# Chunked attention and mixture of experts on one core: one 512 KB load for q and k, earlier stores, routing steps moved behind the maximum

## The chip, the cores and the metric

The kernel runs on one core of a Trainium2 chip. A time is the device time of one execution in microseconds (us). The kernel before was timed three times: 364.58, 366.62 and 370.21 us, a median of 366.62 us.

## The reference

Attention works inside chunks of 64 tokens, for 8 batches, 8 heads, 576 tokens and a head width of 64. Its output, as 4608 rows of 512, goes through a mixture of experts in which every row picks one expert and may skip it:

```python
scores = scale * np.matmul(q_c, k_c.transpose(0, 1, 2, 4, 3))      # 64 x 64 in each chunk
scores = scores - np.max(scores, axis=-1, keepdims=True)
attn = np.exp(scores)
attn = attn / (np.sum(attn, axis=-1, keepdims=True) + 1e-09)
out = np.matmul(attn, v_c)
x = out.transpose(0, 2, 1, 3).reshape(B * S, H * D)                # 4608 x 512

do_compute = x @ w_skip > 0
xc = x[do_compute]
logits = xc @ w_gate                                               # 8 experts
e_idx = np.argmax(logits, axis=1)
gate_w = softmax(logits)[np.arange(len(xc)), e_idx]
for e in range(8):
    mask = e_idx == e
    h = np.maximum(xc[mask] @ w1[e], 0.0)                          # 512 -> 1024
    y[mask] = gate_w[mask, None] * (h @ w2[e])                     # 1024 -> 512
out = x.copy(); out[do_compute] = xc + y
```

## The kernel before, in words

**Attention** works on 36 tiles of 128 rows. The loop over `i` (line 611) is a software pipeline written out by hand: one turn issues a stage of several tiles. TensorE's order in a turn is: transpose of x of tile i-3 (`pe_xtrans`, L282), transpose of the probabilities of tile i-1 (`pe_ptrans`, L244), subtraction of the row maximum for tile i (`pe_sub`, L232, two matmuls that read `mx`), logits of tile i-4 (`pe_logits`, L310 and L311, which read `xh`), matmuls of the routing, scores of tile i+1 (`pe_scores`, L220, 32 matmuls), and probabilities times v of tile i-1 (`pe_pv`, L259, 32 matmuls into `pv`). The PSUM tile `pv` has a single buffer, and so has the bank `xt`.

VectorE normalizes tile i-2 (`ve_norm`: L266, L268, L270, which writes x and thereby frees `pv`), sums the logits (`ve_logits`, L320), does routing steps, and takes the maximum over the scores of tile i+1 (`ve_max`, L226). ScalarE copies the transposed x to `xs` (L294), and GpSimd splits `xs` into the two float16 halves `xh` (a cast, L296, and a subtraction, L297). An engine executes its instructions in the order in which they are written; a wait holds up everything behind it on the same engine.

**Transfers** go through SyncE's one queue, in the order written: q and k of tile i+4 (`load_q`, `load_k`, 256 KB each, into the two halves of one tile `qk`), v (`load_v`, 260 KB), the store of a finished tile of x (`store`, L276), and 16 halves of the first expert's weights (`load_half`, L461) at the turns in `W_TILES`. A load is held back until TensorE has reached a given stage (`paced`), so that transfers keep step with the tiles. The list `others` holds the weight half and the stores of a turn; its length limit (L614) says how many stores a turn may issue.

**Routing** runs on groups of 14, 9 and 13 tiles (`GS`). `route` is a generator whose steps wear a letter and an estimated length: "d" steps are VectorE's, "p" TensorE's, "r" VectorE's reading of a TensorE result. `run_route("d", budget)` issues "d" steps until the budget is spent. The steps make one-hot rows (`oh`, L401, three tiles at a time, beside them `rv` on GpSimd) and in the end, in `finish_records`, the row numbers `reci` (L439).

**Early gathers.** When the first two groups (tiles 0 to 22) are routed and stored, `early_fetch` lets GpSimd gather the first three blocks of rows of the first expert from the output in HBM (`gather`, L475, an indirect DMA each). The gathers wait for `reci` and for the landing of the stores of tiles 0 to 22; the store of tile 22 is the last of them.

**The experts** follow: the first expert's layer 1 is spread over the end of attention (L496 with `pd`), then for each expert layer 1 (L496), layer 2 (L525), the scatter of the results, and the conversion of the next experts' weights to two float16 halves by ScalarE and VectorE (L742, L743).

Of the kernel before, what the change touches and what calls it, by code (L numbers as in the profile page):

```python
# [9 lines left out]
F32 = mybir.dt.float32  # L10
# [8 lines left out]
P = 128  # L19
B, H, S, D = 8, 8, 576, 64  # L20
CH = 64
NTOK = B * S
NT = NTOK // P
DM = H * D
# [13 lines left out]
GS = (14, 9, 13)  # L38
NG = len(GS)
GT = [(g, i, n) for g, n in enumerate(GS) for i in range(n)]  # L40
EARLY_G, EARLY_B = 2, 3
# [6 lines left out]
LOOK = 4  # L48
# [8 lines left out]
EARLY_I = NT - 2  # L57
# [37 lines left out]


@with_exitstack
def moe_attention_kernel(ctx: ExitStack, tc: tile.TileContext, q: bass.AP, k: bass.AP, v: bass.AP, cst: bass.AP, wall: bass.AP, out: bass.AP):
    nc = tc.nc
    halves = (slice(0, CH), slice(CH, P))  # L100

# [5 lines left out]
    ap = apool.__enter__()  # L107
# [8 lines left out]
    T = [dict() for _ in range(NT)]  # L116
# [4 lines left out]
    def paced(ins, at):  # L121
        if at in stage:
            dep = mybir.DependencyInfo(mybir.DependencyClass.Sync, mybir.DependencyReason.DATA)
            tc.add_manual_dep(getattr(ins, "ins", ins), stage[at].name, dep, reason="pace of the transfers")

    def reached(at, ins):
        stage[at] = getattr(ins, "ins", ins)

    def load_q(t, at=None):
        if t < NT:  # L130
            T[t]["qk"] = ap.tile([P, 2, DM], F32, name="qk", bufs=LOOK + 1)
            paced(nc.sync.dma_start(T[t]["qk"][:, 0], q[t]), at)

    def load_k(t, at=None, eng=None):
        if t < NT:
            paced((eng or nc.sync).dma_start(T[t]["qk"][:, 1], k[t]), at)

    def load_v(t, at=None):
        if t < NT:
            T[t]["v"] = ap.tile([P, 2 * KC * VW], F32, name="v", bufs=LOOK + 2)  # L140
            paced(nc.sync.dma_start(T[t]["v"], v[t]), at)

    csb = cpool.tile([P, CCOLS], F32, name="csb")
    load_q(0)
    load_k(0, eng=nc.scalar)
    load_q(1)
    load_k(1)
    load_v(0)
    nc.sync.dma_start(csb, cst)
    load_v(1)  # L150
    load_q(2)
    load_k(2)
    load_v(2)
    load_q(3)
    load_k(3)
    load_v(3)

    ones = cpool.tile([P, P], F16, name="ones")
# [36 lines left out]
    def more_constants():  # L195
        nc.vector.tensor_copy(upper, C("upper"))
        nc.vector.tensor_copy(iota, C("iota"))
        nc.vector.tensor_scalar(wgs[:, :, 0], wg, SR, None, op0=ALU.mult)
        nc.vector.scalar_tensor_tensor(wgs[:, :, 1], wg, SR, wgs[:, :, 0], op0=ALU.mult, op1=ALU.subtract)
        nc.gpsimd.tensor_copy(vals[:, :, 0], C("tok"))  # L200
        nc.gpsimd.tensor_copy(vals[:, :, 2], C("part").to_broadcast([P, NT]))
        nc.gpsimd.memset(ecum[:, 0, :], 0.0)
        nc.gpsimd.memset(rec, 0.0)
# [6 lines left out]


    def pe_scores(t):
        qk = T[t].pop("qk")
        sp = ps_s.tile([P, 2, DM], F32, name="sp")
        for j in range(KC):
            for c in range(2):
                for a in range(2):
                    h = (j % 2) * 4 + (j // 2) * 2 + a
                    w = slice(h * CH, (h + 1) * CH)
                    ins = nc.tensor.matmul(sp[halves[a], c, j * CH:(j + 1) * CH], qk[halves[c], 0, w], qk[halves[c], 1, w], start=(j == 0), stop=False, skip_group_check=True)  # L220
        T[t]["sp"] = sp
        reached("scores", ins)

# [49 lines left out]
    held = []  # L273
# [172 lines left out]
    def run_route(kinds, budget):  # L446
        while routes and routes[0][0][0] in kinds and budget > 0:
            budget -= routes[0][0][1]
            routes[0][0] = next(routes[0][1], None)
            if routes[0][0] is None:  # L450
                routes.pop(0)
# [87 lines left out]
    def on(f, t, *a):  # L539
        if 0 <= t < NT:  # L540
            f(t, *a)
# [26 lines left out]
    def early_xt(m, alloc):  # L568
        blk_xt(xt0[:, :, :, m * P:(m + 1) * P], xgs[m], P, alloc)
# [41 lines left out]
    for i in range(-1, NT):  # L611
        host.clear()
        others = [(load_half, m) for m, t in enumerate(W_TILES) if t == i]
        while held and len(others) < (1 if i < EARLY_I - 5 else 2 if i < NT - LOOK else 4):  # L614
            others.append((store, held.pop(0)))
        run_route("w", 1)
        on(pe_xtrans, i - 3)
        on(ve_norm, i - 2)
        on(ac_xs, i - 3)
        if 0 <= i - 2 < NT:  # L620
            held.append(i - 2)
        if i >= 0:
            on(load_q, i + LOOK, "x")
        on(pe_ptrans, i - 1)
        on(ac_pt, i - 1)
        on(pe_sub, i)
        on(ac_exp, i)
        if i >= 0:
            on(load_k, i + LOOK, "sub")
        on(pe_logits, i - 4)  # L630
        run_route("p", 1)
        on(ve_logits, i - 4)
        run_route("r", 1)
        run_route("d", 750 if i < sum(GS[:EARLY_G]) + 3 else 1000)
        if i in EARLY_AT:
            early_xt(EARLY_AT[i], xt_bank)
        on(pe_scores, i + 1)
        on(ve_max, i + 1)
        for n, (f, t) in enumerate(others):
            f(t, ("scores", None)[n > 0])  # L640
        on(pe_pv, i - 1)
        if i >= 0:
            on(load_v, i + LOOK, "pv")
        if i == 1:
            more_constants()
        if w_pend and (i > W_TILES[FC] or i < W_TILES[FC] and (len(w_pend) > 1 or i > W_TILES[FC - 1])):
            conv_half()
        while i == EARLY_I - 2 and len(ready) == 1:
            host.clear()
            run_route("w", 1)  # L650
            run_route("p", 1)
            run_route("rd", 1 << 30)
        if held and held[0] >= sum(GS[:EARLY_G]):
            early_fetch()
# [170 lines left out]
    for u, (p, bs, offs, n) in enumerate(units):  # L825
# [7 lines left out]
        w, hc = wsets[p], ht  # L833
# [8 lines left out]
        at = 0  # L842
# [57 lines left out]
def lay_out(q, k, v, moe_w_skip, moe_w_gate, moe_w1, moe_w2):  # L900
    nch = S // CH

    def cols(a):
        return np.ascontiguousarray(a.reshape(B, H, nch, CH, D).transpose(0, 2, 4, 1, 3)).reshape(NT, P, DM)


    vv = v.reshape(B, 2, KC, nch, CH, D).transpose(0, 3, 1, 4, 2, 5).reshape(NT, 2, P, KC, D).transpose(0, 2, 1, 3, 4)
    vv = np.concatenate([vv, np.ones((NT, P, 2, KC, 1), np.float32)], axis=4).reshape(NT, P, 2 * KC * VW)
    cst = constants()
    wsg = np.concatenate([moe_w_skip[:, None], moe_w_gate], axis=1)  # L910
    lo, hi = _C["wsg"]
    cst[:, lo:hi] = wsg.reshape(KC, P, NX).transpose(1, 0, 2).reshape(P, -1)
    w1 = moe_w1.reshape(NE, KC, P, FC, P).transpose(0, 3, 2, 1, 4).reshape(NE, FC, P, KC * P)
    w2 = moe_w2.reshape(NE, FC, P, DM)
    wall = np.ascontiguousarray(np.concatenate([w1, w2], axis=3))
    return {"in_q": cols(q), "in_k": cols(k), "in_v": np.ascontiguousarray(vv), "in_cst": cst, "in_wall": wall}


# [12 lines left out]
```

## Time and profile before

| | |
|---|---|
| median of three runs | 366.62 us (364.58 to 370.21) |
| the profiled execution | 364.89 us, its span 363.1 us |
| TensorE busy (PE) | 316.4 us, 87% of the span |
| VectorE (DVE) | 237.5 us, 65% |
| ScalarE (ACT) | 164.7 us, 45% |
| GpSimd (POOL) | 152.4 us, 42% |
| data moved | 81.82 MB, mean 225 GB/s |

All rows of this document come from one profiled execution. PE is TensorE, PEld its weight loads, DVE VectorE, ACT ScalarE, POOL GpSimd, SPq SyncE's queue. "L220" is a line of the kernel. In `[6.18 <-DMA out<-x]` the first number is the idle time of the engine just before the instruction, and behind the arrow stands what ended it; "issue" means that the profile shows nothing that was waited for. [...] Attention ends near 144 us of the span; the rest is the experts.

### The profile page before, as it was taken

To read this page: it belongs to the slowest core of one execution; us is meant where nothing else is said; L and a number is where in the kernel's file an instruction comes from. 1 tells how busy PE (TensorE), PEld (TensorE's weight loads), DVE (VectorE), ACT (ScalarE), POOL (GpSimd) and SP (SyncE) were. 2 spreads that over 40 slices of the span, in tenths; PEclk is the share of its full clock that TensorE was granted. 3 is DMA by queue.
4 is the path that set the end of the run, shared out by engine and by line. 5 is a ranking of instruction groups with operands and counts; after the bars stand their busy time and mean duration, and the time that the engine had idled before them with its cause. 6 is when DMAs were issued, how large, how long until landed. Compare 5 with 4: busy or idle time off the path is not lost.

```text
span 363.1 us, 11291 instructions
## 1 busy us (share of the span) xinstructions
PE 316.4 (87%) x4543; PEld 223.8 (62%) x4543; DVE 237.5 (65%) x526; ACT 164.7 (45%) x335; POOL 152.4 (42%) x179
## 2 busy tenths in 40 slices
PE   7698787788977559989999998999999999999991
PEld 3577676677866547654555543764755857668580
DVE  2455454689697426695556999786777867868320
ACT  2454355444554416424345744463654655456120
POOL 5145576769878287586120026134025023111111
PEclk9999899999999969999999999999999999999996
DMA  8999798989999857816751588767667668663000
GB/s 266 390 277 362 249 327 268 314 258 311 314 301 311 297 167 235 315 43 194 238 170 59 180 265 253 256 199 217 226 204 238 211 209 279 190 217 120 29 25 27
DMA packets 42471, 81.82 MB, mean 225 GB/s; under 512 B 5150, under 2 KB 5150, under 8 KB 42416
## 3 DMA queue, kind: packets, MB, share of 16 engines
q1 hardware_dynamic: 39168, 71.47, 59.9%
q0 software_dynamic: 3104, 9.33, 8.2%
q8 instruction: 37, 0.61, 0.7%
q10 hardware_dynamic: 144, 0.26, 0.2%
q14 instruction: 18, 0.15, 0.1%
HBM read 67.01 MB, written 14.17 MB: 224 GB/s over the span
## 4 chain that ended last, share of the span: by engine, by line
PE 69%; DVE 8%; POOL 6%; issue 5%; DMA 5%; ACT 4%; POOLq 0%; ACTq 0%
PE y L525 26%; PE hp L496 20%; PE sp L220 4%; PE xt L282 4%; PE pv L259 4%; ACT xs L294 3%; PE pd L496 3%; DMA qk<-in_k 3%; PE xq L488 2%; POOL xh L297 2%; PE xt L310 2%; DMA out<-x 2%; PE pt L244 1%; POOL rv L400 1%; DMA xg<-out,reci 1%
## 5 line engine op out<-in xcount | busy, mean ns | idle before, releaser
L525 PE MATMUL y<-wset,ht 128*128 128x512 f16 (+7 forms) x552 | 101.9, 379 | 0.0
L496 PEld LDWEIGHTS <-wset 128*128 128x128 f16 x864 | 73.5, 98 | 24.4 <-issue 3.8
L475 POOL DMA_INDIRECT out<-yo,reci x22 | 24.5, 1115 | 144.2 <-DVE yo L535 123.1
L496 PE MATMUL hp<-xt,wset 128*128 128x288 f16 (+6 forms) x768 | 81.1, 267 | 1.7 <-DVE ht L501 1.1
L525 PEld LDWEIGHTS <-ht 128*128 128x128 f16 (+7 forms) x552 | 45.6, 101 | 46.5 <-issue 2.0
L743 DVE SCALAR_TENSOR_TENSOR wset<-wst,wset 128x512 f16<-128x512 f32 x112 | 71.5, 683 | 1.4 <-ACT wset L742 0.5
L742 ACT ACTIVATE wset<-wst 128x512 f16<-128x512 f32 x112 | 62.9, 620 | 2.2 <-DMA wst<-in_wall 2.2
L500 ACT ACTIVATE ht<-hp 128x288 f16<-128x288 f32 (+6 forms) x64 | 23.5, 371 | 49.9 <-PE hp L496 49.4
L294 ACT ACTIVATE xs<-xt 128x512 f32<-128x512 f32 x33 | 19.7, 596 | 55.9 <-PE xt L282 55.9
L226 DVE TENSOR_REDUCE mx<-sp 128x8 bf16<-128x512 f32 x36 | 24.8, 688 | 25.7 <-PE sp L220 25.7
L501 DVE SCALAR_TENSOR_TENSOR ht<-hp,ht 128x288 f16<-128x288 f32 (+6 forms) x64 | 25.3, 405 | 23.1 <-ACT ht L500 22.0
L297 POOL TENSOR_TENSOR xh<-xs,xh 128x512 f16<-128x512 f32 x33 | 38.5, 1166 | 2.6
L296 POOL CAST xh<-xs 128x512 f16<-128x512 f32 x33 | 20.7, 626 | 32.2 <-ACT xs L294 32.2
L220 PE MATMUL sp<-qk 64*64 64x64 f32 x1152 | 26.7, 230 | 6.8 <-issue 5.8
L475 POOL DMA_INDIRECT xg<-out,reci x22 | 24.5, 1114 | 12.5 <-DMA out<-x 6.2
L259 PE MATMUL pv<-v,pts 64*64 64x65 f32 x1152 | 25.9, 222 | 4.4 <-issue 3.8
L489 ACT ACTIVATE xt<-xq 128x512 f16<-128x512 f32 (+7 forms) x19 | 9.6, 509 | 42.0 <-PE xq L488 42.0
L220 PEld LDWEIGHTS sp<-qk 64*64 64x64 f32 x1152 | 21.4, 139 | 9.9 <-issue 7.3
L270 DVE TENSOR_TENSOR x<-pv,rr 128x512 f32<-128x512 f32 x36 | 24.9, 691 | 1.4 <-DVE rr L268 0.2
L237 ACT ACTIVATE px<-sp 128x512 f32<-128x512 f32 x36 | 21.6, 600 | 8.9 <-PE sp L232 8.9
L259 PEld LDWEIGHTS pv<-v,pts 64*64 64x64 f32 x1152 | 21.9, 137 | 5.7 <-issue 4.6
L535 DVE SCALAR_TENSOR_TENSOR yo<-y,recg,xg 128x512 f32<-128x512 f32 (+7 forms) x23 | 17.1, 742 | 12.2 <-PE y L525 10.9
(122 smaller groups left out, 374.2 us busy)
## 6 DMA issues: line engine op xcount, KB each, us to landing
wst<-in_wall SPq DMA_DIRECT2D x128, 256.0 KB
v<-in_v SPq DMA_DIRECT2D x36, 260.0 KB
qk<-in_q SPq DMA_DIRECT2D x36, 256.0 KB
out<-x SPq DMA_DIRECT2D x36, 256.0 KB
qk<-in_k SPq DMA_DIRECT2D x35, 256.0 KB
xg<-out,reci POOLq DMA_INDIRECT x22, 4.1
out<-yo,reci POOLq DMA_INDIRECT x22, 3.4
qk<-in_k ACTq DMA_DIRECT2D x1, 256.0 KB
```

The costliest lines, as they stand in the source:

```text
L220: ins = nc.tensor.matmul(sp[halves[a], c, j * CH:(j + 1) * CH], qk[halves[c], 0, w], qk[halves[c], 1, w], start=(j == 0), stop=False, skip ...
L226: nc.vector.tensor_reduce(mx, T[t]["sp"][:, :, :KC * CH].rearrange("p c (j s) -> p c j s", s=CH), axis=AX.X, op=ALU.max, negate=True)
L259: ins = nc.tensor.matmul(pv[halves[c], jj, m * VW:(m + 1) * VW], pt[halves[jj], c * 2 + jp, halves[a]], vv[halves[jj], c * KC + m, :], sta ...
L270: nc.vector.tensor_tensor(x.rearrange("p (g m d) -> p g m d", g=2, m=KC), pv[:, :, :, :D], rr.unsqueeze(3).to_broadcast([P, 2, KC, D]), op ...
L294: nc.scalar.activation(xs, T[t].pop("xt"), AF.Copy, scale=SX)
L297: nc.gpsimd.tensor_tensor(xh[:, 1], xs, xh[:, 0], op=ALU.subtract)
L475: ins = nc.gpsimd.indirect_dma_start(**kw)
L496: nc.tensor.matmul(hp, w[:, a, fc, j * P:(j + 1) * P], xt[:, b, j, :n], start=(m == 0), stop=(m == 11))
L501: nc.vector.scalar_tensor_tensor(ht[:, 1, fc, :n], hp, 0.0, ht[:, 0, fc, :n], op0=ALU.max, op1=ALU.subtract)
L525: nc.tensor.matmul(y[c * P // cg:c * P // cg + n], ht[:, a, fc, o:o + n], w[:, b, fc, P * KC:], start=(f == 0 and m == 0), stop=(f == fw - ...
L742: nc.scalar.activation(w[:, 0, fc, r], st[part], AF.Copy, scale=SW)
L743: nc.vector.scalar_tensor_tensor(w[:, 1, fc, r], st[part], SW, w[:, 0, fc, r], op0=ALU.mult, op1=ALU.subtract)
```

## The change

Three edits. First, q and k lie in one input `in_qk` with q and k of a row side by side (4096 bytes), and `load_qk` loads both in one transfer of 512 KB, held back to the stage "sub", as k was; q was held back to the stage "x", somewhat earlier in the turn. Tile 0 is still loaded in two halves on two queues. Second, the limit of one item a turn in `others` ends at turn 26 instead of 29 (`EARLY_I - 8` for `EARLY_I - 5`, `EARLY_I` is 34). Third, `run_route("d", ...)` is called behind `ve_max` instead of ahead of `early_xt`, `pe_scores` and `ve_max`.

```diff
-    def load_q(t, at=None):
+    def load_qk(t, at=None):
         if t < NT:
             T[t]["qk"] = ap.tile([P, 2, DM], F32, name="qk", bufs=LOOK + 1)
-            paced(nc.sync.dma_start(T[t]["qk"][:, 0], q[t]), at)
-
-    def load_k(t, at=None, eng=None):
-        if t < NT:
-            paced((eng or nc.sync).dma_start(T[t]["qk"][:, 1], k[t]), at)
+            paced(nc.sync.dma_start(T[t]["qk"], qk[t]), at)
...
-    load_q(0)
-    load_k(0, eng=nc.scalar)
-    load_q(1)
-    load_k(1)
+    T[0]["qk"] = ap.tile([P, 2, DM], F32, name="qk", bufs=LOOK + 1)
+    nc.sync.dma_start(T[0]["qk"][:, 0], qk[0][:, 0])
+    nc.scalar.dma_start(T[0]["qk"][:, 1], qk[0][:, 1])
+    load_qk(1)
...
-        while held and len(others) < (1 if i < EARLY_I - 5 else 2 if i < NT - LOOK else 4):
+        while held and len(others) < (1 if i < EARLY_I - 8 else 2 if i < NT - LOOK else 4):
             others.append((store, held.pop(0)))
...
-        if i >= 0:
-            on(load_q, i + LOOK, "x")
         on(pe_ptrans, i - 1)
...
         if i >= 0:
-            on(load_k, i + LOOK, "sub")
+            on(load_qk, i + LOOK, "sub")
...
         run_route("r", 1)
-        run_route("d", 750 if i < sum(GS[:EARLY_G]) + 3 else 1000)
         if i in EARLY_AT:
             early_xt(EARLY_AT[i], xt_bank)
         on(pe_scores, i + 1)
         on(ve_max, i + 1)
+        run_route("d", 750 if i < sum(GS[:EARLY_G]) + 3 else 1000)
...
-    return {"in_q": cols(q), "in_k": cols(k), "in_v": ...
+    return {"in_qk": np.ascontiguousarray(np.stack([cols(q), cols(k)], axis=2)), "in_v": ...
```

**SyncE's queue, turns 28 to 31, before.** The numbers in the names tell buffers apart; `x_2062` is x of tile 22, `out_0` the output.

```order
L276 DMA out_0<-x_1615 128x512
L141 DMA v_2518<-in_v 128x520
L132 DMA qk_2539<-in_q 128x512
L136 DMA qk_2539<-in_k 128x512
L276 DMA out_0<-x_1718 128x512
L276 DMA out_0<-x_1809 128x512
L141 DMA v_2603<-in_v 128x520
L132 DMA qk_2621<-in_q 128x512
L136 DMA qk_2621<-in_k 128x512
L276 DMA out_0<-x_1896 128x512
L276 DMA out_0<-x_1979 128x512
L141 DMA v_2700<-in_v 128x520
```

The store of `x_2062` is still four rows further on, behind the loads of `qk_2718`. The same queue in the changed kernel, from turn 27 on, where x of tile 22 is `x_2035`:

```order
L455 DMA wst_2379<-in_wall 128x512
L270 DMA out_0<-x_1695 128x512
L137 DMA v_2399<-in_v 128x520
L132 DMA qk_2431<-in_qk 128x1024
L270 DMA out_0<-x_1785 128x512
L270 DMA out_0<-x_1871 128x512
L137 DMA v_2489<-in_v 128x520
L132 DMA qk_2521<-in_qk 128x1024
L270 DMA out_0<-x_1953 128x512
L270 DMA out_0<-x_2035 128x512
L137 DMA v_2573<-in_v 128x520
L132 DMA qk_2602<-in_qk 128x1024
```

The store of tile 22 is issued in turn 29 instead of turn 31, and a tile has one load for q and k.

**GpSimd, turns 30 to 33, before** (`xh_2715` is tile 28, `xh_2811` tile 29):

```order
L400 TENSOR_TENSOR rv_2475<-ohb_2473,vals_125 128x264
L296 CAST xh_2618<-xs_2616 128x512
L297 TENSOR_TENSOR xh_2618<-xs_2616,xh_2618 128x512
L296 CAST xh_2715<-xs_2713 128x512
L297 TENSOR_TENSOR xh_2715<-xs_2713,xh_2715 128x512
L475 DMA xg_2786<-out_0,reci_129 128x512
L475 DMA xg_2790<-out_0,reci_129 128x512
L475 DMA xg_2794<-out_0,reci_129 128x512
L296 CAST xh_2811<-xs_2809 128x512
```

and in the changed kernel (`xh_2696` is tile 28):

```order
L394 TENSOR_TENSOR rv_2464<-ohb_2462,vals_122 128x264
L290 CAST xh_2588<-xs_2586 128x512
L291 TENSOR_TENSOR xh_2588<-xs_2586,xh_2588 128x512
L469 DMA xg_2671<-out_0,reci_126 128x512
L469 DMA xg_2675<-out_0,reci_126 128x512
L469 DMA xg_2679<-out_0,reci_126 128x512
L290 CAST xh_2696<-xs_2694 128x512
L291 TENSOR_TENSOR xh_2696<-xs_2694,xh_2696 128x512
```

The three gathers stand one tile earlier: ahead of `xh` of tile 28 instead of behind it.

**VectorE, turn 30, before:**

```order
L320 TENSOR_REDUCE lg_2373<-xt_2635 128x9
L420 TENSOR_TENSOR rec_127<-rec_127,xt_2635 128x88
L439 SCALAR_TENSOR_TENSOR reci_129<-rec_127 128x3
L440 TENSOR_TENSOR recg_130<-rec_127 128x3
L441 TENSOR_SCALAR recg_130<-recg_130 128x3
L407 TENSOR_REDUCE es_2658<-eh_2281 128x9
L409 SCALAR_TENSOR_TENSOR ecum_124<-ecum_124,es_2658 128x9
L410 SCALAR_TENSOR_TENSOR addr_126<-val_2278,rank_2382 128x9
L226 TENSOR_REDUCE mx_2679<-sp_2662 128x8
L266 TENSOR_SCALAR rs_2707<-pv_2683 128x8
```

and in the changed kernel:

```order
L314 TENSOR_REDUCE lg_2343<-xt_2604 128x9
L414 TENSOR_TENSOR rec_124<-rec_124,xt_2604 128x88
L220 TENSOR_REDUCE mx_2641<-sp_2624 128x8
L433 SCALAR_TENSOR_TENSOR reci_126<-rec_124 128x3
L434 TENSOR_TENSOR recg_127<-rec_124 128x3
L435 TENSOR_SCALAR recg_127<-recg_127 128x3
L401 TENSOR_REDUCE es_2646<-eh_2270 128x9
L403 SCALAR_TENSOR_TENSOR ecum_121<-ecum_121,es_2646 128x9
L404 SCALAR_TENSOR_TENSOR addr_123<-val_2267,rank_2371 128x9
L260 TENSOR_SCALAR rs_2688<-pv_2652 128x8
```

The maximum of tile 31 moves ahead of the six routing steps, and these now stand between it and the normalization of tile 29. The other turns with "d" steps (17 to 30, except 24 and 25) change in the same way.

## Rows read from the trace of the kernel before

**Rows 1.** Stretches of the span: busy us per engine (instructions), clock, DMA share, GB/s.
```profile
79.00:115.00 36.00, 28.94 (x809) 25.09 (x805) 29.96 (x81) 18.52 (x35) 30.90 (x38) 1.00 0.93 307
123.00:131.00 8.00, 0.75 (x7) 0.36 (x4) 0.64 (x1) 2.20 (x4) 4.96 (x5) 0.84 0.76 241
131.00:144.00 13.00, 11.70 (x264) 10.23 (x265) 6.95 (x19) 7.37 (x14) 10.65 (x13) 0.83 0.58 186
144.00:363.00 219.00, 205.54 (x1554) 129.91 (x1552) 152.07 (x293) 98.06 (x211) 58.71 (x55) 0.99 0.57 183
```

**Rows 2.** Timeline of TensorE: start us, duration us, engine, line, instruction.
```profile
121.15 0.69 PE L220 MATMUL sp<-qk 64*64 64x64 f32 x32
...
122.24 0.66 PE L282 MATMUL xt<-ident,x 128*128 128x128 f32 x4
...
129.92 0.20 PE L310 MATMUL xt<-wgs,xh 128*128 128x18 f16 x1 [6.37 <-POOL xh L296]
131.16 0.19 PE L311 MATMUL xt<-wgs,xh 128*128 128x9 f16 x1 [1.04 <-POOL xh L297]
...
131.44 1.13 PE L220 MATMUL sp<-qk 64*64 64x64 f32 x32
...
133.37 1.11 PE L282 MATMUL xt<-ident,x 128*128 128x128 f32 x4
```

**Rows 3.** Timeline of GpSimd.
```profile
118.00 1.16 POOL L297 TENSOR_TENSOR xh<-xs,xh 128x512 f16<-128x512 f32 x1
125.34 1.26 POOL L475 DMA_INDIRECT xg<-out,reci  x1 [6.18 <-DMA out<-x]
...
129.25 0.62 POOL L296 CAST xh<-xs 128x512 f16<-128x512 f32 x1
129.95 1.15 POOL L297 TENSOR_TENSOR xh<-xs,xh 128x512 f16<-128x512 f32 x1
```

**Rows 4.** Timeline of SyncE's queue (the issue of a transfer, not its length).
```profile
119.09 0.83 SPq L276 DMA_DIRECT2D out<-x  x2
```

**Rows 5.** Timeline of VectorE.
```profile
94.35 0.69 DVE L270 TENSOR_TENSOR x<-pv,rr 128x512 f32<-128x512 f32 x1
...
106.54 2.40 DVE L401 SCALAR_TENSOR_TENSOR oh<-csb,sl 128x384 f16<-128x384 f32 x2
...
115.25 1.08 DVE L439 SCALAR_TENSOR_TENSOR reci<-rec 128x3 int32<-128x3 f32 x1
...
116.43 0.17 DVE L441 TENSOR_SCALAR recg<-recg 128x3 f32<-128x3 f32 x1
...
117.00 0.69 DVE L226 TENSOR_REDUCE mx<-sp 128x8 bf16<-128x512 f32 x1
```

**Rows 6.** Timeline of TensorE, other places.
```profile
38.72 0.58 PE L220 MATMUL sp<-qk 64*64 64x64 f32 x24 [2.09 <-issue]
...
39.69 1.11 PE L282 MATMUL xt<-ident,x 128*128 128x128 f32 x4
...
95.86 0.57 PE L259 MATMUL pv<-v,pts 64*64 64x65 f32 x25
```

**Rows 7.** Waits of TensorE from 60 to 120 us: total us, times, longest us.
```profile
PE sp L232 <- DVE mx L226: 6.4, 7, 1.2
```

**Rows 8.** Waits of TensorE over the whole span.
```profile
PE sp L220 <- issue: 5.8, 3, 2.1
PE pv L259 <- issue: 3.8, 5, 1.5
...
PE sp L220 <- DMA qk<-in_k: 0.9, 1, 0.9
```

**Rows 9.** DMA queues over the span: packets, MB, share of 16 engines' time.
```profile
q1 hardware_dynamic: 39168, 71.47, 59.9%
q0 software_dynamic: 3104, 9.33, 8.2%
```

**Rows 10.** DMA queues from 17 to 120 us.
```profile
q8 instruction: 19, 0.31, 1.2%
```

More of the change, by code (lines that the diff above doesn't have):

```diff
@@ L97, in moe_attention_kernel @@
 @with_exitstack
-def moe_attention_kernel(ctx: ExitStack, tc: tile.TileContext, q: bass.AP, k: bass.AP, v: bass.AP, cst: bass.AP, wall: bass.AP, out: bass.AP):
+def moe_attention_kernel(ctx: ExitStack, tc: tile.TileContext, qk: bass.AP, v: bass.AP, cst: bass.AP, wall: bass.AP, out: bass.AP):
     nc = tc.nc
@@ L150, in moe_attention_kernel @@
     load_v(1)
-    load_q(2)
-    load_k(2)
+    load_qk(2)
     load_v(2)
-    load_q(3)
-    load_k(3)
+    load_qk(3)
     load_v(3)
@@ L212, in pe_scores @@
     def pe_scores(t):
-        qk = T[t].pop("qk")
+        qt = T[t].pop("qk")
         sp = ps_s.tile([P, 2, DM], F32, name="sp")
@@ L219, in pe_scores @@
                     w = slice(h * CH, (h + 1) * CH)
-                    ins = nc.tensor.matmul(sp[halves[a], c, j * CH:(j + 1) * CH], qk[halves[c], 0, w], qk[halves[c], 1, w], start=(j == 0), stop=False, skip_group_check=True)
+                    ins = nc.tensor.matmul(sp[halves[a], c, j * CH:(j + 1) * CH], qt[halves[c], 0, w], qt[halves[c], 1, w], start=(j == 0), stop=False, skip_group_check=True)
         T[t]["sp"] = sp
@@ L915, in lay_out @@
     wall = np.ascontiguousarray(np.concatenate([w1, w2], axis=3))
-    return {"in_q": cols(q), "in_k": cols(k), "in_v": np.ascontiguousarray(vv), "in_cst": cst, "in_wall": wall}
+    return {"in_qk": np.ascontiguousarray(np.stack([cols(q), cols(k)], axis=2)), "in_v": np.ascontiguousarray(vv), "in_cst": cst, "in_wall": wall}
 def kernel(**inputs):
```

## The prediction

> **What bounds the kernel now.** I first cut the span into stretches [rows 1]. From 144 us to the end TensorE is busy 205.54 of 219 us: the experts run at TensorE's speed, and whatever attention gives up ahead of them comes off the end. From 79 to 115 us TensorE is busy 28.94 of 36 us, with GpSimd at 30.90 and VectorE at 29.96, so nearly three engines share that limit. From 123 to 131 us TensorE works 0.75 of 8 us. That hole is the first thing to explain.
>
> TensorE's timeline [rows 2] shows it: the scores of tile 33 start at 121.15, and then the logits of tile 29 wait 6.37 us for the cast that makes `xh`, and 1.04 us more for the subtraction behind it. The scores of tile 34 start only at 131.44. GpSimd's timeline [rows 3] tells why the cast was late: GpSimd finished tile 28 at 118.00 + 1.16 = 119.16 and then stood 6.18 us in front of the first early gather, which waited for a store. SyncE issued the stores of tiles 22 and 23 at 119.09 [rows 4], so the last store that the gathers need had only just left. Its landing, 6 us later with the gather's own start, ended the wait; the three gathers then kept GpSimd from 125.34 to 129.25, 3.91 us.
>
> Two smaller things bound attention elsewhere: seven waits of `pe_sub` for the row maximum, 6.4 us between 60 and 120 us [rows 7], and eight waits "issue", 9.6 us, in the middle of scores or of `pv` [rows 8].
>
> **The change, part by part.** *Stores two turns earlier.* The store of tile 22 now leaves in turn 29, ahead of the loads of turns 30 and 31, so its landing falls before `reci` is ready. The gathers then wait for `reci`. Before, `reci` started at 115.25 and took 1.08 us [rows 5]. Now the maximum (0.69) goes first: 115.25 + 0.69 + 1.08 = 117.0. The gathers take 3.91 us, to 120.9. But they now stand ahead of `xh` of tile 28, not behind it. Cast and subtraction take 129.25 to 131.10, 1.85 us [rows 3], so this `xh` is complete at 122.8 instead of 119.16. The logits of tile 28 wait for it, and the scores of tile 33 follow 131.44 - 131.16 = 0.28 us behind [rows 2], at 123.1: 1.9 us later than before. That is the price of the move. `xh` of tile 29 is then ready at 122.8 + 1.85 = 124.7, while its logits come 2.4 us behind the scores (121.15 to 129.92 - 6.37), at 125.5: no wait. A turn without those waits is 131.44 - 121.15 - 6.37 - 1.04 = 2.9 us, so the scores of tile 34 start at 126.0 instead of 131.44: **-5.4 us**. Bounds: if the store lands late enough to bring back half of the 6.18 us, -2.3; if `reci` takes 0.17 us, as a step of the same size behind it does [rows 5], -6.3. Turns 26 to 28 get one more store each. SyncE's queue has room: TensorE waited for a q or k load once in the whole run, 0.9 us [rows 8]. If the cover went, a store would cost a 256 KB share of the queue's 0.93 busy time, some 0.7 us a turn by q1's packets [rows 9].
>
> *TensorE's clock.* [...] The new wait is 1.9 us long. After the wait of 2.09 us at 38.72 the transposes at 39.69 took 1.11 us, so the clock did fall there [rows 6]. [...] I lean to the upper clock, since that earlier wait followed others, but GpSimd is busy 10.65 of the 13 us [rows 1] and returns some: **-1.5 us**.
>
> *Routing behind the maximum.* All seven waits of 6.4 us go in name. What is late next is the normalization, which now stands behind the routing steps and frees the only `pv` buffer. In a turn without routing the normalization ends at 94.35 + 0.69 = 95.04 and `pv` starts at 95.86 [rows 5, 6]: 0.8 us of slack. Two `oh` steps of 2.40 us [rows 5] exceed it by 1.6 us, where the old order cost 6.4 / 7 = 0.9 us a wait [rows 7]. Turns with two `oh` steps therefore lose, those with short ones gain up to their 0.8 to 1.2 us. Also GpSimd, 86% busy from 79 to 115 us, gets its `rv` inputs 0.69 us later, as these VectorE steps now come behind the maximum. Bounds: -6.4 (all gone) and +2.1 (the three turns with a pair of `oh` steps at +0.7, nothing elsewhere). I take **-1.0**, near the second end, since GpSimd's row is the nearest limit. `early_xt` in turns 34 and 35 moves past no "d" step and costs nothing.
>
> [...]
>
> *One load for q and k.* 256 packets of 2048 bytes become 128 of 4096 a tile. Row q1 gives 0.599 x 16 x 363.1 us / 39168 = 89 ns for a mean packet of 1825 bytes; row q0, the gathers and scatters, gives 153 ns for 3006 bytes [rows 9]. Time per byte is 49 and 51 ps: the same. Bounds: same time per byte, 0; same time per packet, 128 x 89 ns / 16 = 0.7 us of DMA time a tile, 25 us over 35 tiles, of which only what TensorE waits for counts, the 0.9 us above. I take **-0.1**. q leaves one stage later in the turn, a transposition of 0.66 us [rows 2]; loads run four tiles ahead, and that lead covers it. One issue a tile less on SyncE's queue frees nothing that is waited for.
>
> **Sum.** -5.4 - 1.5 - 1.0 - 0.1 = -8.0 us. Against the profiled execution that is 364.89 - 8.0 = 356.9; the median of the runs is 1.73 us above that execution, so the forecast in terms of the median is 366.62 - 8.0 = **358.6 us**.
>
> **The rivals.**
>
> *A smaller gain: the wait moves rather than goes.* GpSimd still waits for a store (the 256 KB more a turn in turns 26 to 28 make landings later), or the new wait of 1.9 us brings the lower clock, and routing gives nothing. For it: DMA is already at 0.93. Against it: two turns of lead. -2.3 to -5, 363 us.
>
> *A larger gain: DMA paces attention.* DMA is busy 0.93 from 79 to 115 us; if that were the limit, packets twice as large and the maximum off the path could return TensorE's whole 36 - 28.94 = 7.1 us there [rows 1], 6 beyond what I took: 352.5 us. Against it: a load was waited for once, and time per byte is flat [rows 8, 9]. [...]
>
> *Slower: TensorE's instruction fetch.* The eight "issue" waits break off a run of equal matmuls that wait for nothing, as at 38.72 [rows 6], and 19 instruction transfers pass between 17 and 120 us [rows 10]; I read the one as the other. A load row now holds a DMA engine 153 instead of 89 ns, so a fetch queued behind such rows comes later. If the other 11 fetches began to cost the mean of 1.2 us, that is +13.2: 371.8 us. It beats the gain from the seventh further wait on (8.0 / 1.2). Against it: the bytes on the queue are the same. [...]
>
> *The change doesn't do what it says:* the gathers find another late operand and the hole stays: 366 us, and then the new order gains nothing either.
>
> **How the numbers follow.** A measurement here tells about 2% from no change, 7.3 us, so the border is 359.3. Forecast 0.56, within 356 to 361.5, three fifths of it below the border (0.33); smaller gain 0.18; larger gain 0.14; hole stays 0.06; slower 0.06, half of it by over 2%. Faster by over 2%: 0.33 + 0.14 = 0.47; within: 0.23 + 0.18 + 0.06 + 0.03 = 0.50; slower: 0.03. The range 353 to 364.5 leaves out the last two cases and part of the larger gain.
>
> **What would show it.** Right: GpSimd's first early gather starts near 117 us of the old time scale, its wait for the store is gone, and TensorE's one wait for `xh` there is about 2 us in front of the logits of tile 28. The waits of `pe_sub` for `mx` go, and waits of `pv` for the normalization or of the logits for `xh` appear instead in turns 20 to 23 and 28. The q1 queue moves the same bytes in fewer packets, with about the same share of busy time. Wrong: the gather's wait on a store above 3 us, "issue" waits far above 9.6 us, or TensorE's idle time from 79 to 115 us halved.

## The result, and the profile after

The changed kernel takes 357.21 us (median of 4 runs, 355.63 to 358.76); the kernel before took 365.60 us beside it. The ratio is 0.975 with a 95% interval of 0.971 to 0.980, that is -9.0 us (-7.4 to -10.6). Forecast was -8.0. The profiled execution took 357.59 us with a span of 355.9 us, 7.2 us less than before. In this document medians are over all executions, while ratios leave out executions more than 1.5% above the fastest of their kernel, among them one of two by heads that took 522 us at a clock of 0.56. All rows come from one profiled execution of a kernel.

**Stretches of the span**, at the times of [rows 1]; columns as there:

```profile
79.00:115.00 36.00, 29.14 (x800) 25.21 (x790) 27.09 (x77) 16.09 (x31) 29.93 (x36) 0.95 0.91 308
...
123.00:131.00 8.00, 7.51 (x224) 6.64 (x216) 4.06 (x11) 4.31 (x8) 5.21 (x7) 0.89 0.81 268
131.00:144.00 13.00, 12.22 (x175) 9.02 (x165) 8.23 (x22) 8.50 (x16) 9.76 (x11) 1.00 0.85 274
```

The hole from 123 to 131 us is gone: TensorE works 7.51 of 8 us there, where it worked 0.75. From 79 to 115 us its busy time hardly changed (29.14 for 28.94).

**GpSimd's timeline**, which answers to [rows 3]:

```profile
113.59 1.16 POOL L291 TENSOR_TENSOR xh<-xs,xh 128x512 f16<-128x512 f32 x1
116.34 1.26 POOL L469 DMA_INDIRECT xg<-out,reci  x1 [1.60 <-DMA out<-x]
117.91 1.01 POOL L469 DMA_INDIRECT xg<-out,reci  x1 [0.31 <-issue]
119.23 1.01 POOL L469 DMA_INDIRECT xg<-out,reci  x1 [0.31 <-issue]
120.24 0.62 POOL L290 CAST xh<-xs 128x512 f16<-128x512 f32 x1
120.95 1.15 POOL L291 TENSOR_TENSOR xh<-xs,xh 128x512 f16<-128x512 f32 x1
```

The first gather starts at 116.34 instead of 125.34 (forecast: 117.0), and its wait for a store is 1.60 instead of 6.18 us. The store is still what comes last. VectorE's `reci` was ready 1.6 us before the gather:

```profile
113.98 0.69 DVE L220 TENSOR_REDUCE mx<-sp 128x8 bf16<-128x512 f32 x1 [0.33 <-PE sp L214]
114.58 0.18 DVE L433 SCALAR_TENSOR_TENSOR reci<-rec 128x3 int32<-128x3 f32 x1
```

**TensorE's timeline** at the same place, which answers to [rows 2]:

```profile
113.22 0.69 PE L214 MATMUL sp<-qk 64*64 64x64 f32 x32
...
116.10 0.69 PE L214 MATMUL sp<-qk 64*64 64x64 f32 x32
116.67 0.52 PE L253 MATMUL pv<-v,pts 64*64 64x65 f32 x13
117.63 0.50 PE L253 MATMUL pv<-v,pts 64*64 64x65 f32 x16 [0.45 <-issue]
118.48 0.33 PE L253 MATMUL pv<-v,pts 64*64 64x65 f32 x3 [0.35 <-issue]
120.51 0.60 PE L276 MATMUL xt<-ident,x 128*128 128x128 f32 x4 [1.69 <-issue]
...
122.15 0.19 PE L305 MATMUL xt<-wgs,xh 128*128 128x9 f16 x1
...
122.44 1.13 PE L214 MATMUL sp<-qk 64*64 64x64 f32 x32
...
126.26 0.69 PE L214 MATMUL sp<-qk 64*64 64x64 f32 x32
```

The scores of tile 34 start at 126.26 instead of 131.44 (forecast 126.0). The wait ahead of them has another name than forecast: TensorE stands 0.80 us in two breaks in the middle of `pv` and 1.69 us in front of the transposes, all named "issue". But the late `xh` of tile 28 ends at the same place. It is complete at 120.95 + 1.15 = 122.10; the first logits matmul that needs its subtracted half starts at 122.15, and the scores of tile 33 follow 0.29 us behind, as forecast. Without the stops they could not have started earlier either. They then take 1.13 us, where those of tile 34 take 0.69: the granted clock, as a share of TensorE's full speed, is 0.50 from 121.4 to 124.8 us and 1.00 from 126.26 to 131.

**TensorE's waits from 60 to 120 us**, which answer to [rows 7]:

```profile
PE xt L276 <- issue: 2.4, 2, 1.7
PE xt L305 <- POOL xh L291: 2.1, 2, 1.1
PE pv L253 <- issue: 1.6, 3, 0.8
```

No wait of the subtraction for the maximum is left of 6.4 us. In its place "issue" grew (5.3 us in all, 4.2 before), and so did waits for `xh`, `xs` and `px` (4.4 us, 1.1 before). The load queue moves the same bytes in fewer packets and about the same time, as forecast [rows 9]:

```profile
q1 hardware_dynamic: 34128, 71.47, 60.2%
```

The starts of the scores mark the tiles (the maxima don't serve here, since the third edit itself moves them ahead of the routing steps). Tile 31's scores now start at 113.22 (above); before it was

```profile
114.78 0.69 PE L220 MATMUL sp<-qk 64*64 64x64 f32 x32
```

So in this execution 1.6 us come from ahead of tile 31, where 1.1 were forecast for the order and the load together. From tile 31 to tile 34 it takes 126.26 - 113.22 = 13.04 us instead of 131.44 - 114.78 = 16.66: 3.6 us come from the hole. The other 2.0 of the 7.2 come from behind. That called for taking the edits apart.

### The profile page after: what moved, and what is told of

The parts are those of the page before. It is cut to its first block, busy times and chain, and to the rows that moved or that the text cites. A ratio compares the mean times of both kernels' runs of the same rounds, so it can differ in the third digit from the quotient of the medians.

```text
span 355.9 us, 11195 instructions
## 1 busy us (share of the span) xinstructions
PE 319.3 (90%) x4543; PEld 225.7 (63%) x4543; DVE 234.6 (66%) x526; ACT 164.2 (46%) x335; POOL 152.7 (43%) x179
## 3 DMA queue, kind: packets, MB, share of 16 engines
q1 hardware_dynamic: 34128, 71.47, 60.2%
## 4 chain that ended last, share of the span: by engine, by line
PE 68%; DVE 10%; issue 5%; ACT 5%; POOL 5%; DMA 4%; SPq 1%; ACTq 0%; POOLq 0%; DVEq 0%
PE y L519 24%; PE hp L490 20%; PE sp L214 5%; PE xt L276 4%; PE pv L253 4%; ACT xs L288 3%; DVE wset L735 3%; PE pd L490 3%; PE xq L482 2%; DMA qk<-in_qk 2%; PE pt L238 2%; PE xt L304 2%; POOL xh L291 2%; DMA wst<-in_wall 1%; DVE ht L495 1%
## 5 line engine op out<-in xcount | busy, mean ns | idle before, releaser
L253 PEld LDWEIGHTS pv<-v,pts 64*64 64x64 f32 x1152 | 22.7, 142 | 7.5 <-issue 5.1
L276 PE MATMUL xt<-ident,x 128*128 128x128 f32 x132 | 22.8, 293 | 4.6 <-issue 4.1
L238 PE MATMUL pt<-ident,px 128*128 128x128 f32 x144 | 23.5, 286 | 2.3 <-issue 2.2
```

What stands on the lines that cost most here:

```text
L238: nc.tensor.transpose(pt[:, j, :], px[:, j * P:(j + 1) * P], ident)
L253: ins = nc.tensor.matmul(pv[halves[c], jj, m * VW:(m + 1) * VW], pt[halves[jj], c * 2 + jp, halves[a]], vv[halves[jj], c * KC + m, :], sta ...
L276: ins = nc.tensor.transpose(xt[:, j, :], x[:, j * P:(j + 1) * P], ident)
```

## The experiments

All but the changed kernel were timed in five rounds against the kernel before.

| kernel | store limit | order | q and k | median us | ratio to before (95%) | us |
|---|---|---|---|---|---|---|
| changed kernel | new | new | one load | 357.21 | 0.975 (0.971 to 0.980) | -9.0 |
| stores alone | new | old | two loads | 360.66 | 0.987 (0.982 to 0.993) | -4.7 |
| order alone | old | new | two loads | 369.94 | 1.008 (1.003 to 1.012) | +2.8 |
| load alone | old | old | one load | 359.47 | 0.985 (0.980 to 0.989) | -5.6 |
| order and load | old | new | one load | 361.98 | 0.987 (0.982 to 0.992) | -4.8 |
| stores and load | new | old | one load | 356.84 | 0.976 (0.972 to 0.981) | -8.6 |
| q later | old | old | two loads, both behind the subtraction | 364.56 | 0.995 (0.991 to 1.000) | -1.8 |
| 2 KB rows | old | old | one load of 256 rows | 360.28 | 0.985 (0.978 to 0.992) | -5.5 |
| load earlier | old | old | one load, at the old place of q | 361.24 | 0.982 (0.977 to 0.987) | -6.8 |
| two by heads | old | old | two loads, a wait for each | 360.55 | 0.981 (0.975 to 0.987) | -6.9 |
| two by heads, joint wait | old | old | two loads, one wait for both | 366.97 | 1.007 (1.001 to 1.014) | +2.7 |
| shift | old | old | two loads, 64 matmuls ahead | 364.08 | 0.990 (0.984 to 0.996) | -3.8 |
| gathers spread | new | old | one load | 355.13 | 0.967 (0.962 to 0.972) | -12.1 |

The last column is the ratio less 1 times the median of before in the same comparison (365.60 to 366.87 us).

### The three edits, each alone

*Stores alone.* The one edit in the kernel before:

```diff
-        while held and len(others) < (1 if i < EARLY_I - 5 else ...
+        while held and len(others) < (1 if i < EARLY_I - 8 else ...
```

> The kernel before with nothing changed but the store limit (8 turns instead of 5 ahead of EARLY_I). Theory A, the prediction's: the hole in front of the gathers is nearly the whole gain. The first gather starts near 117 us instead of 125.3, the scores of tile 34 near 126 to 126.5 instead of 131.4, and the time is 5.5 to 7 us below the kernel before, some 359.5 us. Rival B, the new order of VectorE carries it: the gathers then still start 3 us or more late behind a routing step, and this kernel gains less than 3.5 us. Rival C, the gain needs the merged loads (landings too late without them): the gather still waits for a store for over 3 us and the gain is under 3 us.

The gather's wait shrank to 1.44 us and it started at 118.63 us:

```profile
118.63 1.26 POOL L475 DMA_INDIRECT xg<-out,reci  x1 [1.44 <-DMA qk<-in_k]
```

(The row names a load of k, which the gather does not read; which landing ended this wait is not shown.) The scores of tile 34 started at 127.50, later than the 126 to 126.5 of theory A. Counted from those of tile 31, at 115.66, that is 11.84 us instead of 16.66.

-4.7 us (-2.7 to -6.6): theory A for the mechanism, a little under its range of 5.5 to 7 in size. The merged loads are not needed for it.

*Order alone.* Only `run_route("d", ...)` moved behind `ve_max`:

```diff
-        run_route("d", 750 if i < sum(GS[:EARLY_G]) + 3 else 1000)
         if i in EARLY_AT:
             early_xt(EARLY_AT[i], xt_bank)
         on(pe_scores, i + 1)
         on(ve_max, i + 1)
+        run_route("d", 750 if i < sum(GS[:EARLY_G]) + 3 else 1000)
```

> The kernel before with nothing changed but routing's VectorE steps behind the maximum. Theory A: the waits of the subtraction for the maximum go (7.2 us in sum down to 1 or less), the scores of tile 31 start about 1 us earlier than 114.8, but the hole in front of the gathers keeps its end or moves by the same 1 us: 0 to -1.5 us. Rival B: the order carries the gain, -3 us or more. Rival D, the GpSimd inputs come later and the single pv buffer is freed later: +1 us or more.

+2.8 us (1.2 to 4.4): rival D by its number. First the waits of TensorE in this kernel from 60 to 120 us, then GpSimd's wait for the gate and its first gather:

```profile
PE sp L220 <- issue: 4.0, 3, 1.6
PE pv L259 <- issue: 3.4, 3, 1.4
PE xt L311 <- POOL xh L297: 1.7, 2, 1.1
```

```profile
106.15 0.21 POOL L362 CAST vals<-gate 128x9 f16<-128x9 f32 x1 [2.78 <-DVE gate L361]
...
128.39 1.26 POOL L475 DMA_INDIRECT xg<-out,reci  x1 [6.73 <-DMA v<-in_v]
```

The 6.4 us of waits for the maximum went, as expected, and came back: "issue" grew from 4.2 (3.7 + 0.5 in the same stretch of before) to 7.4, and waits for `xh`, `xs` and `px` from 1.1 to 3.5. The scores of tile 31 started at 117.28, not 1 us earlier than 114.8. Up to tile 28 nothing was lost (its scores started at 102.11, before at 102.82); from there to tile 31 it took 15.17 us instead of 11.96, with two stops named "issue" of 1.62 and 1.44 us, against one of 0.26. GpSimd stood 2.78 us for the gate, where it had stood 0.84: the gate's steps now stand behind a maximum whose scores the first of these stops had broken off. That the gate is what cost the time is not shown. The gathers started 3.05 us later than before. With the other edits in place the order's price was not seen: order and load against load alone 0.987 to 0.985, the changed kernel against stores and load 0.975 to 0.976, both within the intervals.

*Load alone.* The part of the diff on `load_qk`, its calls and its input, with nothing else.

> The kernel before with nothing changed but q and k in one transfer. Theory A: time per byte is flat, loads were never waited for but 0.9 us: within 0.5 us of the kernel before. Rival C, larger rows make the DMA engines faster: -2 us or more, and stores and v loads land over 0.5 us sooner. Rival E, longer rows delay instruction fetch: the waits that the profile names issue grow by 2 us or more, and the time by 1 us or more.

-5.6 us (-3.9 to -7.3): theory A fell. The hole was untouched in this kernel:

```profile
118.80 1.26 POOL L469 DMA_INDIRECT xg<-out,reci  x1 [5.41 <-DMA out<-x]
```

*Order and load.*

> The changed kernel with the old store limit (5 turns ahead of EARLY_I), that is, the new order and the merged loads together. Theory A: -1 to -2 us against the kernel before; the first gather again waits about 6 us for a store and the lower clock follows the hole. Rival B: -3 us or more without the stores.

-4.8 us, rival B's number, but from the load, not from the order. The first gather waited 5.21 us, as theory A had it.

*Stores and load*, the changed kernel with the order put back:

> The changed kernel with routing's VectorE steps put back ahead of the maximum, that is, merged loads and the new store limit alone. Theory A': the four runs so far add up (loads -5.6, stores -4.7, order +2.8), so without the order it is 2 to 3 us faster than the changed kernel: 354 to 356 us, ratio to before 0.967 to 0.972. Rival B': the order costs only where the gathers wait (in the order-only run GpSimd stood 2.8 us for the gate behind the maximum); with the stores early it costs nothing, and the time is that of the changed kernel, 357 to 358 us. Rival C': it is slower than the changed kernel, as the prediction's -1.0 us for the order would have it: 358 to 359 us.

-8.6 us against -9.0 of the changed kernel: rival B'. The three single effects sum to -4.7 + 2.8 - 5.6 = -7.5 us; the changed kernel's -9.0 (-7.4 to -10.6) does not contradict that.

### Why the merged load gains

What the load-alone kernel lost were stops named "issue". From 28 to 82 us TensorE stopped 8.4 us for them before (three times in the scores, 5.8, and twice in `pv`, 2.6); here:

```profile
PE xt L276 <- issue: 1.7, 2, 1.1
PE pv L253 <- issue: 1.7, 1, 1.7
PE sp L214 <- issue: 0.2, 1, 0.2
```

These stops sit at fixed places of TensorE's program. In four kernels with two loads, one falls behind the 8th of the 32 score matmuls of tile 10, whenever that is. The row of before is in [rows 6]; the others, of stores alone, order alone and q later:

```profile
37.87 0.58 PE L220 MATMUL sp<-qk 64*64 64x64 f32 x24 [1.55 <-issue]
```

```profile
37.96 0.58 PE L220 MATMUL sp<-qk 64*64 64x64 f32 x24 [1.00 <-issue]
```

```profile
38.06 0.58 PE L220 MATMUL sp<-qk 64*64 64x64 f32 x24 [1.53 <-issue]
```

Counted along TensorE's matmuls, the stops ahead of the gathers lie some 127 apart (126 to 128) or a multiple of it, but for one in order alone (113.02 us) and one in shift (11.64), and each ends 2.2 to 3.5 us, most 2.3 to 2.6, behind the start of a 16 KB packet of the instruction queue. For the stop at 38.72 of before, that queue shows no packet from 33 to 36.1 us and one that starts between 36.1 and 36.2 (this row is of that tenth of a microsecond):

```profile
q8 instruction: 1, 0.02, 69.8%
```

By this spacing and these packets I take them for waits for TensorE's next instructions; no row names what ended them. The packets of that queue are of 16 KB (37 in the span of before, 0.61 MB), and 127 matmuls with their weight loads are 254 instructions, a block in what follows. In the changed kernel the stop of 1.69 us above is one of them (253 matmuls behind the stop ahead of it, 2.55 us behind the start of a packet); the two breaks in `pv` are not. Over the whole span of before, 9.6 us of these stops were counted [rows 8].

Three kernels asked first what in the merged load spares them.

*q later:* two loads, but q issued just ahead of k.

```diff
-            on(load_q, i + LOOK, "x")
...
+            on(load_q, i + LOOK, "sub")
             on(load_k, i + LOOK, "sub")
```

> The kernel before; q and k stay two transfers with rows of 2048 bytes, but q is issued where the merged load is, just ahead of k behind the subtraction, instead of behind the transposition of x. Theory P (place): TensorE stops every 126 or 127 matmuls for its next 16 KB of instructions, and what the merged load changed is when the loads enter the queues against that; then this kernel gains 3 us or more of the 5.6. Theory S (size): the longer rows let the instruction packet through sooner; then this one gains under 1.5 us, and waits named issue stay near 8 us between 28 and 82 us.

*2 KB rows:* one transfer, from an input where q and k lie apart.

```diff
-            paced(nc.sync.dma_start(T[t]["qk"], qk[t]), at)
+            paced(nc.sync.dma_start(T[t]["qk"], qk[t].rearrange("c p d -> p c d")), at)
```

> As the load-only kernel, one transfer a tile at the same place, but q and k lie apart in memory, so that it has 256 rows of 2048 bytes instead of 128 of 4096. Theory S (size of the rows): the gain of 5.6 us goes, under 1.5 us is left, and q1 has some 39000 packets. Theory N (number of transfers or their place): the gain stays, 4 us or more.

*Load earlier:* the merged load, written behind the transpose of x.

```diff
-            on(load_qk, i + LOOK, "sub")
+            on(load_qk, i + LOOK, "x")
```

> As the load-only kernel, rows of 4096 bytes in one transfer, but issued where q alone was issued before, behind the transposition of x. Theory S: the gain stays, 4 us or more. Theory P: the gain changes by over 2 us with the place (less, if the old place of q was the bad one).

The 256 shorter rows (38608 packets on q1) kept the gain, -5.5 us, so it is not the rows' size. The old place of q kept it, -6.8 us, and q's new place without the merge gave -1.8 us (-0.1 to -3.5), so it is not the place, at least not for most of it. Theory S fell with 2 KB rows, theory P with load earlier. The -1.8 us of q later lies between what the two theories had asked for, under 1.5 us and 3 or more.

What was left was the number of transfers, or the wait for them. In the kernel before, the first score matmul of a tile waits for two transfers, and TensorE's weight-load side has a wait instruction at that line. Its rows, first of the kernel before, then of load alone:

```profile
L220 PEldq EVENT_SEMAPHORE  x36: 51/51/674, 4.3 to 136.1; - x36
```

```profile
L214 PEldq EVENT_SEMAPHORE  x4: 51/51/51, 4.5 to 15.5; - x4
```

(Columns: line, engine, instruction, count, shortest, median and longest ns, first and last start.) One a tile before, four in all with one load.

*Two by heads* separates the two: again two transfers of 256 KB with rows of 2048 bytes, but heads 0 to 3 of q and k in one and heads 4 to 7 in the other, so that the first score matmul waits for one and the ninth for the other.

```diff
-            T[t]["qk"] = ap.tile([P, 2, DM], ...)
-            paced(nc.sync.dma_start(T[t]["qk"], qk[t]), at)
+            T[t]["qk"] = ap.tile([P, 2, 2, DM // 2], ...)
+            for h in range(2):
+                paced(nc.sync.dma_start(T[t]["qk"][:, h], qk[t][:, h]), at)
...
-    w = slice(h * CH, (h + 1) * CH)
-    ... qt[halves[c], 0, w], qt[halves[c], 1, w]
+    w = slice(h % 4 * CH, (h % 4 + 1) * CH)
+    ... qt[halves[c], h // 4, 0, w], qt[halves[c], h // 4, 1, w]
```

> As the load-only kernel, but each tile's q and k come in two transfers of 128 rows of 2048 bytes, as in the kernel before: heads 0 to 3 of q and k in one, heads 4 to 7 in the other, both issued behind the subtraction. The first matmul of the scores then waits for one transfer and the ninth for the other, so TensorE needs no instruction of its own for a second wait, which the kernel before has once a tile. Theory X (TensorE's program): the merged load gained because that instruction goes, which moves the places at which TensorE's 16 KB blocks of instructions end; then the gain stays, 4 us or more, and the stops named issue fall at the same matmuls as in the load-only kernel (602, 856, 1111, 1238 ...). Theory Y (number of transfers): the gain goes, under 1.5 us is left.

-6.9 us (-4.8 to -9.1): theory X; the gain stayed with two transfers. The stops fell at the matmuls of load alone (603, 858, 1112 and 1240 in the count of this trace, 603, 857, 1112 and 1239 there). Then the same kernel with the joint wait put back, and nothing else:

```diff
+            T[t]["both"] = getattr(ins, "ins", ins)
...
+                    if "both" in T[t]:
...
+                        tc.add_manual_dep(getattr(ins, "ins", ins), T[t].pop("both").name, dep, ...)
```

> As the two-transfer kernel with a wait for one transfer at a time (heads 0 to 3, heads 4 to 7; ratio 0.981), but the first matmul of the scores waits for both transfers, as in the kernel before. Transfers, rows, bytes and places are those of the two-transfer kernel; only the wait differs, and with it one more instruction of TensorE a tile. Theory X (that instruction, or the joint wait, is what the split loads cost): the gain goes, the ratio to before is 0.993 or above, and the time between the maxima of tiles 2 and 28 goes from 88.0 back to 92 us or more. Rival Y' (something else of the split loads, such as q and k lying apart): the gain stays, ratio 0.987 or below, 90 us or less between the maxima.

+2.7 us (0.2 to 5.2): the gain was gone, as theory X had it. By the medians it is 366.97 against 366.30 us, so that it is slower than the kernel before is hardly shown. Between the two kernels the bytes, the rows, the transfers and their places are equal. The wait instruction, first with a wait for each transfer, then with the joint wait:

```profile
L215 PEldq EVENT_SEMAPHORE  x3: 51/51/51, 9.1 to 15.3; - x3
```

```profile
L217 PEldq EVENT_SEMAPHORE  x35: 51/51/372, 7.5 to 136.7; - x35
```

Their traces from the maximum of tile 2 to that of tile 28, in the same order:

```profile
10.39:98.42 88.03, 74.45 (x2183) 64.84 (x2176) 60.80 (x170) 45.39 (x86) 59.38 (x71) 1.00 0.96 323
```

```profile
10.51:105.80 95.29, 77.82 (x2187) 68.09 (x2179) 61.92 (x171) 45.59 (x87) 59.49 (x71) 0.96 0.91 301
```

and TensorE's waits in the second of them:

```profile
PE sp L217 <- issue: 5.1, 4, 2.0
PE pv L259 <- issue: 5.0, 5, 1.9
PE sp L232 <- DVE mx L226: 3.5, 4, 1.1
PE pt L244 <- issue: 1.5, 1, 1.5
PE sp L217 <- DMA qk<-in_qk: 0.3, 1, 0.3
```

The 7.26 us between them are 11.6 - 7.9 = 3.7 us more of "issue" (3.4 + 2.3 + 1.6 + 0.6 with single waits) and 77.82 - 74.45 = 3.4 us more of TensorE's busy time at a mean granted clock of 0.96 instead of 1.00. The loads themselves were waited for 0.3 us. So the merged load gains because the joint wait goes. All traces agree: from the scores of tile 2 to those of tile 28 the six kernels with the joint wait take 91.7 to 94.0 us, the eight without it 86.9 to 90.5. The gain comes as less "issue" in load alone too, 5.2 us against 9.3 before, between the maxima of tiles 2 and 28. The clock does not belong to it: load alone ran there at a mean of 0.96, the kernel before at 0.98.

*Shift* tried whether the instruction works through the places at which the blocks end:

```diff
+    for _ in range(64):
+        nc.tensor.matmul(warm[:, :8], ones, zeros[:, :8], start=True, stop=True)
     pe_warm(10)
```

> The kernel before with 64 matmuls of 8 columns put ahead of its warm-up, while TensorE waits for the first loads: every later matmul stands 64 places further on, half a block of instructions. Part of the answer is the same by both theories: the stops named issue move to other places of the program, 64 matmuls earlier in the work, and still come 2.3 to 2.6 us behind the start of a 16 KB packet. Theory X (the places decide): the time between the maxima of tiles 2 and 28, 93.3 to 94.1 us in four kernels with split loads, changes by 2 us or more, and the total with it. Theory Y: it stays within 1 us, and the total within 1.5 us of the kernel before.

The stops moved as they should. The total fell by 3.8 us (1.6 to 6.1), which speaks for the places; the time between the maxima of tiles 2 and 28 was 92.5 us, 0.9 less than before, which speaks against them. The two profiled executions differ by 0.9 us only (363.98 and 364.89), so no trace shows where the 3.8 us lie. They came with the joint wait in place, so part of what such an edit gains may be where it happens to put the ends of the blocks; a shifted kernel with the merged load was not run. How one 51 ns instruction a tile lengthens the stops stays open. Its own time is not it: a turn without a stop takes 2.79 us with it and without it (tiles 13 to 14, 48.95 to 51.74 before, 46.52 to 49.31 in two by heads).

### A version that beats both

The three gathers in a row cost GpSimd 3.9 us in one place. Here they go one a turn, from turn 30 on, in the kernel with stores and load and the old order:

```diff
     def early_fetch():
-        for m in range(min(EARLY_B, ready[-1])):
+        m = len(xgs)
+        if m < min(EARLY_B, ready[-1]):
             fetch(m, P * sum(GS[:EARLY_G]))
```

> Merged loads, the new store limit, the old order of VectorE, and the three early gathers issued one a turn instead of all behind turn 30. GpSimd then holds up the xh of tile 28 by one gather instead of three. Theory: the waits of the logits for xh in turns 31 and 32 shrink by up to 2.6 us, attention ends 1 to 2.6 us sooner, 354 to 356 us. Rival: the second and third gather hold up the next two xh by 1.3 us each, which are waited for as well, or the first wait for the store is what bounds: within 0.7 us of the kernel without the order, 356.8 us.

-12.1 us (-10.2 to -14.0), in the range of the theory; its interval for the ratio, 0.962 to 0.972, lies almost wholly below that of the changed kernel, 0.971 to 0.980. Against the kernel without the spread it is 1.7 us by the medians and 3.5 by the ratios; the three were not timed side by side, but each against the kernel before. Its GpSimd:

```profile
112.24 1.26 POOL L469 DMA_INDIRECT xg<-out,reci  x1 [1.71 <-DMA out<-x]
...
115.54 1.04 POOL L469 DMA_INDIRECT xg<-out,reci  x1 [0.16 <-issue]
...
118.61 1.04 POOL L469 DMA_INDIRECT xg<-out,reci  x1 [0.16 <-issue]
```

From the scores of tile 31 to those of tile 34 it takes 119.05 - 109.00 = 10.05 us; the kernel without the spread took 125.22 - 111.97 = 13.25, the changed kernel 13.04. `pv` is no longer broken up there, and the clock stays at 1.00 from 108 to 127 us. But the next turn gives most of this back:

```profile
123.94 0.17 PE L304 MATMUL xt<-wgs,xh 128*128 128x18 f16 x1 [1.44 <-ACT xs L288]
```

ScalarE's copy to `xs` stood behind its conversion of a weight half, which had waited 3.07 us for that half to land. Up to the scores of tile 35 the gain over the kernel without the spread is (128.94 - 111.97) - (125.14 - 109.00) = 0.8 us. Of the 3.9 us between the two profiled executions 2.7 lie between tiles 2 and 28, ahead of the edit. So the time is measured, but how much of it the spread earned is not shown.

## Why the prediction was right, and where it was not

The time and its direction were right: 8.0 us forecast, 9.0 (7.4 to 10.6) measured. Of the four terms, one carried what it was said to carry.

- **Stores two turns earlier, -5.4 us: right in the mechanism, and in its times with luck.** Alone they gave -4.7 (-2.7 to -6.6). In the changed kernel the gathers started at 116.34 (forecast 117.0) and the scores of tile 34 at 126.26 (126.0), but 1.6 us of that came from ahead of tile 31. Counted from tile 31's scores, 3.6 of the 5.4 us came, and two steps were off. The first gather came 0.9 us later than forecast (3.1 us behind these scores instead of 2.2): it still waited 1.60 us for its store, where it was to wait for `reci`, which took 0.18 us instead of 1.08 (0.18 in all three kernels with the new order, 0.86 to 1.08 in all others). And the turn behind the late `xh` had a granted clock of 0.50 up to 124.8 us and took 126.26 - 122.44 = 3.8 us instead of 2.9. The price of the late `xh` itself was as forecast, though stops named "issue" hid its name.
- **Clock, -1.5 us: wrong for this execution.** I leaned to the upper clock. No run shows the -1.5 us: the scores of tile 33 took 1.13 us at a granted clock of 0.50, as those of tile 34 did before (0.50 from 131.44 to 135.00 us); the stretch from 123 to 131 us has 0.89. The lower clock came a turn earlier and ended sooner: from 131 us on it is 1.00 against 0.83 [rows 1].
- **Routing behind the maximum, -1.0 us: wrong sign.** Alone it cost 2.8 us (1.2 to 4.4), in the full change nothing that can be measured. The place that I named as next to be late, the normalization, shows no wait. The waits for the maximum went, but TensorE's stops named "issue" and its waits for `xh`, `xs` and `px` took up what they gave back. GpSimd's later inputs had been named as a limit, and its gate was late (2.78 us); but its price was left below the upper bound of +2.1, and that it is the cause is not shown.
- **One load for q and k, -0.1 us: wrong, the largest miss.** It gave -5.6 us (-3.9 to -7.3), outside the bounds that I set. They went by bytes and packets, and on these they were right: time per byte stayed flat (0.602 x 16 x 355.9 us / 71.47 MB is 48 ps a byte, against 49), and halving the rows again changed nothing (-5.5 against -5.6 us). The step that failed is that the edit was costed as a transfer alone. It also took a wait instruction a tile off TensorE, and that was not in the sum: 4.1 us less "issue" from tile 2 to tile 28 in load alone.

The two misses, +1.0 to +3.8 us on the order and -5.5 us on the load, partly cancel, so the total is nearer than its parts, by luck. The larger rival, 352.5 us, had the load as its lever, but by DMA speed; q1 and its share (60.2% against 59.9) say no. The slower rival had the right place, the "issue" stops, which I read as TensorE's instruction fetch, with the wrong sign: I feared that longer rows would hold up the fetch. How long a fetch is held, no row shows. From the maximum of tile 2 to that of tile 28, "issue" fell from 9.3 us (5.8 in the scores, 3.5 in `pv`) to 7.3 (3.6 in `pv`, 2.2 and 0.7 in the transposes, 0.8 in the scores).

## What to carry to other kernels

Cost an edit of a transfer on the engine that waits for it too: here a first matmul that waited for two transfers had a wait instruction (36 of them before, 35 in two by heads with the joint wait) that went with one transfer (4 left) or one wait for each of two matmuls (3 left), and that was worth as much as the whole hole in front of the gathers (-5.6 us for load alone, -4.7 for stores alone; how much elsewhere is not shown). Where "issue" stops recur at a fixed count of instructions, here 254 or a multiple of it, a removed wait can be worth less than its row: in order alone 6.4 us of waits went and "issue" grew by 3.2. Mark tiles by an instruction that the edit leaves in its place. And spread work that an engine does in a block over turns in which it has slack, as the gathers here, and look at the turn behind it before you count the gain.

## What the runs showed of the hardware

- TensorE's stops named "issue": some 127 matmuls apart in the program or a multiple of it, up to 2.8 us each (in the shifted kernel), and 7.9 against 11.6 us of them in two kernels that differ in one wait a tile.
- Three indirect gathers in a row came with short breaks in the middle of TensorE's `pv`. In stores alone, while the gathers ran from 118.63 to 122.53:

```profile
120.73 0.27 PE L259 MATMUL pv<-v,pts 64*64 64x65 f32 x1 [0.33 <-issue]
121.35 0.46 PE L259 MATMUL pv<-v,pts 64*64 64x65 f32 x9 [0.35 <-issue]
122.18 0.36 PE L259 MATMUL pv<-v,pts 64*64 64x65 f32 x5 [0.37 <-issue]
122.94 0.64 PE L282 MATMUL xt<-ident,x 128*128 128x128 f32 x4 [0.39 <-issue]
```

The changed kernel and the one with stores and load show them too, the one with the gathers spread does not. VectorE stood as well: in stores alone its maximum of tile 32 came 2.3 us after the scores that it reads had ended (119.21 + 0.69 = 119.90), and the row names no engine or transfer ("remote"):

```profile
122.24 0.69 DVE L226 TENSOR_REDUCE mx<-sp 128x8 bf16<-128x512 f32 x1 [2.31 <-remote]
```

So VectorE stood there too, not TensorE alone. What they waited for was not settled.
